# A tiny Exp as ScalarE's first work, with the loads of x and gate_w issued behind it

## Chip, cores and metric

One Trainium2 chip (trn2), one of its cores. The metric is device microseconds of one execution, lower is better. Each kernel is executed several times; of most kernels here some runs are 1.1 to 1.6 us longer than the rest (state "slow"). A profile is one further execution, with its own span; the time of an execution is about 1.7 us longer than the span of its profile.

## The reference, cut to what matters

One decode step mixes two branches with a scalar gate: attention of 32 heads over the last 4096 positions of a K and V cache with 8 heads, and a gated MLP.

```python
x = A_x                                              # (1, 1, 512)
g = _sigmoid((x * gate_w).sum(-1, keepdims=True))
a = attention(x @ wq, k_cache[:, :, -4096:], v_cache[:, :, -4096:]) @ wo
b = (_sigmoid(x @ w_gate) * (x @ w_up)) @ w_down
return g * a + (1 - g) * b
```

Everything is bf16 and read once: wq 4 MB, K and V 8 MB each, wo 4 MB, the three MLP matrices 1.8 MB each. x and gate_w have 1 KB each.

## The kernel before

SyncE issues all big loads in one fixed order, ScalarE the two small ones. A tile pool takes room in SBUF in the order in which its tiles are named, and the pools stand one behind the other, `const` first.

```python
const = ctx.enter_context(tc.tile_pool(name="const", bufs=1))
big = ctx.enter_context(tc.tile_pool(name="big", bufs=1))     # wq, later wo
blk = ctx.enter_context(tc.tile_pool(name="blk", bufs=4))     # four K tiles, later four V tiles
w14 = ctx.enter_context(tc.tile_pool(name="w14", bufs=3))     # w_gate, w_up, w_down
# ... ktp, work and the PSUM pools
xr = const.tile([1, 2, D], BF16, name="xr")
nc.scalar.dma_start(xr[:, 0, :], A_x[0, :, :])
nc.scalar.dma_start(xr[:, 1, :], gate_w.rearrange("(o n) -> o n", o=1))
dq = nc.sync
wq_sb = big.tile([P, DC, HQ * DH], BF16, name="wq_sb", tag="big")
dq.dma_start(wq_sb[:], wq_v)
# ... K, w_gate, w_up, V, wo, w_down, all on dq in this order
spare = const.tile([1, 1], F32, name="spare")
for _ in range(4):
    nc.vector.memset(spare[:], 0.0)
# ... x transposed on TensorE, then the gate:
nc.vector.tensor_tensor(gpr[:], xr[:, 0, :], xr[:, 1, :], op=ALU.mult)
nc.vector.tensor_reduce(gsum[:], gpr[:], axis=AX.X, op=ALU.add)
nc.tensor.matmul(z_ps[:], lhsT=ones_f[0:1, :], rhs=gsum[:], start=True, stop=True)
nc.scalar.activation(gex[:], z_ps[:], AF.Exp, scale=-1.0)     # the first Exp
# ... q = x @ wq on TensorE, K transposed on VectorE, scores, softmax, P V, output projections
```

## Time and profile before

| | before |
|---|---|
| median of 6 runs | 80.65 us (80.44 to 81.89) |
| span of the profile | 78.7 us |
| DMA engines, queue of SyncE | 92.9% of the span, 30.67 MB |
| TensorE, VectorE, ScalarE busy | 67%, 49%, 14% |
| table load for Exp | 1.53 to 2.81 us |
| first Exp | 10.54 us |

To read it: the DMA stream is the bound, and compute follows it at a distance of about a microsecond at the end. The prediction shows the lines.

### The profile page before, as it was taken

What the parts mean: (1) busy time and instruction counts of PE and PEld (TensorE: products, weight loads), DVE (VectorE), ACT (ScalarE), POOL (GpSimd) and SP (SyncE); (2) the same over time, 40 slices, a digit from 0 to 9 for tenths busy, and PEclk for the clock granted to TensorE, in tenths of its full rate; (3) what the DMA queues carried; (4) which work ended last, traced back from release to release, by engine and by line L of the source; (5) the groups of instructions that cost most, each with busy time, mean ns of one, the idle gap of its engine ahead of it and who ended that gap; (6) DMA issues with size and microseconds to landing.
All of it is one profiled execution on the core that took longest, in us unless ns stands there. A gap on an engine that the chain in (4) does not pass through costs nothing.

```text
span 78.7 us, 798 instructions
## 1 busy us (share of the span) xinstructions
PE 52.5 (67%) x314; PEld 23.6 (30%) x314; DVE 38.8 (49%) x52; ACT 10.9 (14%) x20; POOL 3.3 (4%) x10
## 2 busy tenths in 40 slices
PE   0200094999905788898887307999996799567650
PEld 0200041344302333333332202344341345345420
DVE  1600920029869999999986349962000000690020
ACT  2400000247651000000002191000000002000010
POOL 7900000000000000000000000000000000000000
PEclk9999999999999999999999995699999999999997
DMA  7779799999999999999999999999999999999710
GB/s 184 300 316 533 316 483 391 408 425 458 441 408 416 425 474 416 386 437 417 438 410 426 441 416 441 408 433 441 416 433 433 424 425 433 416 391 409 290 42 1
DMA packets 2616, 30.71 MB, mean 390 GB/s; under 512 B 307, under 2 KB 438, under 8 KB 822
## 3 DMA queue, kind: packets, MB, share of 16 engines
q1 hardware_dynamic: 2608, 30.67, 92.9%
q8 instruction: 2, 0.03, 0.2%
q10 hardware_dynamic: 6, 0.00, 0.0%
HBM read 30.67 MB, written 0.00 MB: 390 GB/s over the span
## 4 chain that ended last, share of the span: by engine, by line
DMA 93%; SPq 2%; PE 1%; DVE 1%; issue 0%
DMA wd_sb<-in_B_w_down_dram 36%; DMA kn<-in_A_k_cache_dram 32%; DMA vv<-in_A_v_cache_dram 24%; SPq L84 2%; PE a_ps L290 1%; DVE res L341 1%; SPq L80 0%
## 5 line engine op out<-in xcount | busy, mean ns | idle before, releaser
L299 PE MATMUL pv_ps<-vv,eT 128*32 128x512 bf16 x64 | 15.9, 405 | 4.1 <-DVE eT L271 2.8
L227 PE MATMUL S_ps<-kT,qbig 128*128 128x512 bf16 x64 | 15.2, 378 | 5.0 <-DVE qbig L216 2.8
L188 DVE STREAM_TRANSPOSE kT<-kn 128x2048 f32<-128x2048 f32 x8 | 17.8, 2282 | 0.0
L227 PEld LDWEIGHTS <-qbig 128*128 128x128 bf16 x64 | 6.1, 97 | 14.1 <-issue 4.2
L299 PEld LDWEIGHTS <-eT 128*32 128x32 bf16 x64 | 6.2, 102 | 12.9 <-issue 4.2
L200 PE MATMUL q_ps<-wq_sb,xT 128*128 128x512 bf16 x32 | 8.8, 442 | 1.2 <-DMA wq_sb<-in_A_wq_dram 1.2
L318 DVE TENSOR_TENSOR oT<-o_ps,rb 128x32 bf16<-128x32 f32 x1 | 0.2, 191 | 13.5 <-PE o_ps L316 13.5
L205 DVE STREAM_TRANSPOSE qtT<-q_sb 128x512 f32<-128x512 f32 x4 | 2.7, 700 | 6.9 <-ACT q_sb L202 6.9
L182 PE MATMUL S_ps<-ident,other 2*128 2x512 bf16 x4 | 2.0, 611 | 5.8 <-DVE other L140 5.8
L202 ACT CAST q_sb<-q_ps 128x512 bf16<-128x512 f32 x8 | 4.7, 585 | 7.0 <-PE q_ps L200 7.0
L200 PEld LDWEIGHTS <-xT 128*128 128x128 bf16 x32 | 3.5, 111 | 6.8 <-issue 4.2
L290 PE MATMUL a_ps<-wo_sb,oY 128*1 128x256 bf16 x64 | 3.8, 272 | 1.5 <-DMA wo_sb<-in_A_wo_dram 1.2
L290 PEld LDWEIGHTS <-oY 128*1 128x1 bf16 x64 | 2.7, 83 | 3.1 <-issue 1.4
L271 DVE STREAM_TRANSPOSE eT<-e_sb 128x1024 bf16<-128x1024 bf16 x2 | 2.4, 1224 | 1.9 <-ACT e_sb L269 1.9
L254 ACT ACTIVATE sge<-gu_ps 128x448 f32<-128x448 f32 x1 | 0.5, 543 | 18.9 <-PE gu_ps L243 18.9
L309 ACT COPY pv_sb<-pv_ps 128x512 f32<-128x512 f32 x1 | 0.6, 585 | 17.7 <-PE pv_ps L299 17.7
L341 DVE CAST res<-a_ps 1x256 bf16<-1x256 f32 x1 | 0.4, 412 | 5.2 <-PE a_ps L290 5.2
L281 DVE RECIPROCAL sg<-sge 128x448 f32<-128x448 f32 x1 | 3.0, 2952 | 0.0
L165 DVE TENSOR_TENSOR gpr<-xr 1x512 f32<-1x512 bf16 x1 | 0.7, 679 | 4.6 <-DMA xr<-in_gate_w_dram 4.6
L249 DVE TENSOR_REDUCE pm<-S_ps 128x1 f32<-128x1024 f32 x2 | 2.4, 1208 | 0.9 <-PE S_ps L227 0.9
L290 PE MATMUL a_ps<-wd_sb,hT 128*1 128x256 bf16 x28 | 2.1, 271 | 0.8 <-DMA wd_sb<-in_B_w_down_dram 0.8
L148 PE MATMUL xt_ps<-ident,xr 1*128 1x1 bf16 x4 | 0.3, 165 | 3.5 <-POOL ident L126 3.5
(62 smaller groups left out, 31.0 us busy)
## 6 DMA issues: line engine op xcount, KB each, us to landing
kn<-in_A_k_cache_dram SPq DMA_DIRECT2D x4, 2048.0 KB, 27.2
vv<-in_A_v_cache_dram SPq DMA_DIRECT2D x4, 2048.0 KB, 19.1
wq_sb<-in_A_wq_dram SPq DMA_DIRECT2D x1, 4096.0 KB
wo_sb<-in_A_wo_dram SPq DMA_DIRECT2D x2, 2048.0 KB
wg_sb<-in_B_w_gate_dram SPq DMA_DIRECT2D x1, 1792.0 KB
wu_sb<-in_B_w_up_dram SPq DMA_DIRECT2D x1, 1456.0 KB
wd_sb<-in_B_w_down_dram SPq DMA_DIRECT2D x1, 1024.0 KB
wd_sb<-in_B_w_down_dram SPq DMA_DIRECT2D x1, 384.0 KB
```

What stands on the lines that cost most here:

```text
L84: dq.dma_start(t[:, n0:n1, :].rearrange("p n d -> p (n d)"), cache[0, 2 * a:2 * a + 2, SBASE:SBASE + W, :] .rearrange("y (x n) d -> x y n ...
L182: nc.tensor.matmul(S_ps[u // 2][:, u % 2, :], lhsT=other[:].rearrange("p o y u -> p (o y u)"), rhs=ident[0:2, 0:2].rearrange("p (o y) -> p ...
L188: nc.vector.transpose(t[:].bitcast(F32), kn[a][:, v * KB:(v + 1) * KB, :] .rearrange("p n d -> p (n d)").bitcast(F32))
L200: nc.tensor.matmul(q_ps[:], lhsT=xT[:, c:c + 1].to_broadcast([P, P]), rhs=wq_sb[:, c, ks], start=(c == 0), stop=(c == DC - 1))
L202: nc.scalar.copy(q_sb[:, ks], q_ps[:])
L205: nc.vector.transpose(qtT[:].bitcast(F32)[:, kq], q_sb[:].bitcast(F32)[:, kq])
L227: nc.tensor.matmul(S_ps[v][:, hb, :], lhsT=q_st[:, a, dhi, :, t], rhs=k_v[:, hb * 16:(hb + 1) * 16, dhi, :, t], start=False, stop=(a == HP ...
L249: nc.vector.tensor_reduce(pm2[:, v:v + 1], S_ps[v][:].rearrange("p a b -> p (a b)"), axis=AX.X, op=ALU.max)
L271: nc.vector.transpose(eT[:, :, v * KB:(v + 1) * KB, :].rearrange("p a n r -> p n a r"), e_sb[:, v, :].rearrange("p (n a r) -> p n a r", a= ...
L281: nc.vector.reciprocal(sg[:], sge[:])
L290: nc.tensor.matmul(a_ps[32 * i:32 * i + 1, i, 0:HN], lhsT=lhsT, rhs=rhs[:, i * HN:(i + 1) * HN], start=start, stop=stop)
L299: nc.tensor.matmul(pv_ps[32 * a:32 * a + 32, :, :], lhsT=eT[:, a, 4 * m:4 * m + 4, :].rearrange("p n r -> p (n r)"), rhs=vv[a][:, 4 * m:4 ...
```

## The change

ScalarE is put under the written order from the start, and its first instruction is an Exp on a one-element tile, so that the table of Exp is loaded while nothing else is to be done. The loads of x and gate_w come behind it.

```diff
+    ctx.enter_context(tc.manual_schedule(engines={mybir.EngineType.Activation}))
+    warm = const.tile([1, 1], F32, name="warm")
+    nc.vector.memset(warm[:], 0.0)
+    nc.scalar.activation(warm[:], warm[:], AF.Exp)
     xr = const.tile([1, 2, D], BF16, name="xr")
     nc.scalar.dma_start(xr[:, 0, :], A_x[0, :, :])
     nc.scalar.dma_start(xr[:, 1, :], gate_w.rearrange("(o n) -> o n", o=1))
@@
-    for _ in range(4):
+    for _ in range(3):
         nc.vector.memset(spare[:], 0.0)
```

## The prediction

> **What bounds the kernel now.** I began with the slices of the page and its queue table, to see which resource has no room left.
>
> ```profile
> DMA  7779799999999999999999999999999999999710
> ...
> q1 hardware_dynamic: 2608, 30.67, 92.9%
> ```
>
> The first line gives the busy share of the 16 DMA engines in 40 slices of the 78.7 us span: 7 to 9 tenths up to slice 6, then 9 without a gap until slice 37. In the second line the queue that SyncE fills carries 30.67 MB and takes 92.9% of the engines. No compute engine is near this (PE 67%, DVE 49%). Next came the chain of waits in order of time (start us, duration, what).
>
> ```profile
> 46.84 28.67 DMA wd_sb<-in_B_w_down_dram
> 75.51 0.04 issue
> 75.55 0.66 PE a_ps L290 x6
> 76.20 0.40 DVE res L341
> ```
>
> The last piece of compute, 0.66 us of matmuls and a 0.40 us copy, follows the landing of the last part of w_down at 75.51 us. Before it the chain consists of transfers alone (93% of the span on the page). So the end is set by how long one queue needs for its bytes, plus about 1.1 us of compute and the store. A change at the start matters only if it makes this stream start earlier or later, makes it run dry, or holds compute up for longer than compute now waits for data.
>
> To see which work the change touches, I read the timeline of the first 20 us (start, duration, engine, line, tiles, count, and in brackets the idle time before it with its releaser).
>
> ```profile
> 0.73 0.38 SPq L80 DMA_DIRECT2D wq_sb<-in_A_wq_dram  x1
> 0.74 0.51 ACTq L74 DMA_DIRECT2D xr<-in_A_x_dram  x1
> ...
> 1.28 0.21 ACTq L75 DMA_DIRECT2D xr<-in_gate_w_dram  x1
> ...
> 1.53 1.28 ACT L170 ACT_TABLE_LOAD   x1 [1.53 <-PEq L358]
> 2.03 1.25 DVE L153 COPY xp<-xr 1x64 bf16<-1x64 bf16 x2 [0.83 <-DMA xr<-in_A_x_dram]
> ...
> 7.83 0.68 DVE L165 TENSOR_TENSOR gpr<-xr 1x512 f32<-1x512 bf16 x1 [4.56 <-DMA xr<-in_gate_w_dram]
> ...
> 9.55 0.14 DVE L158 CAST xT<-xt_ps 128x4 bf16<-128x4 f32 x1
> ...
> 9.68 0.60 PE L182 MATMUL S_ps<-ident,other 2*128 2x512 bf16 x1 [5.75 <-DVE other L140]
> ...
> 10.37 1.44 PE L182 MATMUL S_ps<-ident,other 2*128 2x512 bf16 x3
> 10.54 0.17 ACT L170 ACTIVATE gex<-z_ps 128x1 f32<-128x1 f32 x1 [7.73 <-PE z_ps L168]
> ...
> 12.98 7.25 PE L200 MATMUL q_ps<-wq_sb,xT 128*128 128x512 bf16 x25 [1.17 <-DMA wq_sb<-in_A_wq_dram]
> ```
>
> Three things are to be seen. First, the table load for Exp already stands at 1.53 us, right behind the two small loads, and ends at 2.81; the first Exp starts at 10.54 and the page of waits puts its 7.7 us of idle time on z_ps, a matmul. The load has 7.7 us to spare. Second, the x load, issued at 0.74, lets VectorE start at 2.03, while gate_w, issued half a microsecond later, releases gpr only at 7.83. Third, everything between gate_w and the first q matmul runs in VectorE's and TensorE's order: gpr, its sum, two small setup instructions and xT, then four matmuls that end at 11.81 (10.37 + 1.44). The q matmuls then wait 1.17 us for wq, until 12.98.
>
> Why gate_w takes 6.3 us (1.49 to 7.83) is told by the trace's packet records. Both loads are one packet of 1024 bytes and one of 4 bytes, on one DMA engine. The data packet of x went at 1.64, before that engine began on wq at 1.76. The data packet of gate_w went at 6.21, behind three wq packets of 32 KB (2.0, 1.23 and 1.22 us), and its 4-byte packet at 7.47, exactly one wq packet later.
>
> For the slack further on I read the later timeline.
>
> ```profile
> 27.70 14.67 SPq L84 DMA_DIRECT2D vv<-in_A_v_cache_dram  x4
> ...
> 61.58 2.97 PE L299 MATMUL pv_ps<-vv,eT 128*32 128x512 bf16 x13 [1.28 <-DMA vv<-in_A_v_cache_dram]
> ...
> 71.38 1.91 PE L290 MATMUL a_ps<-wo_sb,oY 128*1 128x256 bf16 x32 [1.22 <-DMA wo_sb<-in_A_wo_dram]
> ...
> 73.90 1.46 PE L290 MATMUL a_ps<-wd_sb,hT 128*1 128x256 bf16 x22 [0.61 <-DMA wd_sb<-in_B_w_down_dram]
> ...
> 75.55 0.61 PE L290 MATMUL a_ps<-wd_sb,hT 128*1 128x256 bf16 x6 [0.19 <-DMA wd_sb<-in_B_w_down_dram]
> ```
>
> Here PE waits for data at vv (1.28 us), at the second half of wo (1.22), and at two parts of w_down (0.61 and 0.19).
>
> **What the Trainium skill says.** "ScalarE: Activation LUTs", section "What ACT_TABLE_LOAD costs", gives about 1283 ns for the load and about 1380 ns of drain; the trace has 1283 ns for the load and cannot show the drain, as ScalarE has nothing to do behind it. "DMA: Bandwidth & Descriptors", section "Queues, rings and completion order", says that each DMA engine takes turns between queues at packet granularity; the one wq packet between gate_w's two packets agrees, the three before the first one are more than a single turn, and I take the measured three. "Perfetto Trace Analysis", section "DVE / Act Engine Instruction (TENSOR_ADD, Activation, etc)", says that the sequencer pushes an instruction into a wait queue and is then ready for the next; whether the loads therefore pass the running table load is shown nowhere in this trace. "TensorE: Matmul & The Clock Gate", Part 1, puts the slow phase of a cold TensorE at about 3.4 us of activity; here q matmuls are 0.43 us apart from 12.98 to 16.35, 3.37 us, and about 0.22 apart afterwards.
>
> **The change, part by part.** The diff looks like a gain of one table load. I compared the instruction orders of the two builds as well.
>
> Removed: one of four VectorE memsets (four take 0.40 us at 0.79) in place of which the memset of the warm tile comes. Net zero, and VectorE has 0.83 us of idle time there. The table load of gex moves to the front; as the Exp at 10.54 waited for a matmul, nothing is gained on that side.
>
> Added: one 1x1 Exp, estimated at 0.17 us after the 128x1 Exp of gex (171 ns).
>
> Moved: the loads of x and gate_w. If the sequencer goes on while the table loads, x is issued just after the memset, at about 1.0 us. If it waits for the Exp, at 0.74 + 1.28 + 0.17, about 2.2. If a drain of 1.38 us is paid as well, at about 3.6. Issue takes 0.51 us and the packet went 0.39 us behind it (1.25 to 1.64). So x reaches its DMA engine at about 1.9, 3.1 or 4.5. In none of these is it ahead of wq, whose first packet there started at 1.76. With the running packet and two more ahead, as for gate_w, the first two cases put the data of x at 6.2 and the third at 7.45. From there one wq packet (1.22) lies between each two of the four small packets: the last, of gate_w, comes 3.7 us after the first, at 9.9 or 11.1, and lands 0.36 us later (7.47 to 7.83): 10.3 or 11.5. That is 2.5 to 3.7 us later than now.
>
> From gate_w's landing to the end of the setup matmuls is 11.81 - 7.83 = 3.98 us, so q can start at 14.3 or 15.5, against 12.98: 1.3 or 2.5 us late, since 1.17 us are swallowed by the wait for wq. Part of this returns. The setup matmuls now join the q matmuls without the 1.17 us gap, so I estimate that the 3.37 us of slow pace begin with them: in the first case from 12.15, until 15.5, when some 3 q matmuls are done, and the other 29 at 0.216 need 6.3 us, to about 21.8. Now the last q matmul ends at about 21.7. So compute behind q is late by 0.1 us, in the other case by about 1.3, and if the warm-up doesn't help, by the full 1.3 or 2.5.
>
> What lies behind q has room for this: 1.28 + 1.22 + 0.61 + 0.19 = 3.3 us of waits for data on PE. So the end of compute doesn't move.
>
> Does the stream move? The order of SyncE's queue is unchanged. In the build, the semaphores that DMAs share in turn rotate by one: wq now comes before x, so the load of w_up, which waited for x, now waits for wq. Its issue goes from 4.47 to about 12.95. At that moment four K loads of 2 MB and 1.8 MB of w_gate are still queued, about 24 us at the measured 0.41 to 0.43 MB per us. The V loads, issued at 27.70 and later, also wait for VectorE to free the K buffers. The first such transpose ends 24.52 + 2.27 = 26.8, so 0.9 us of lateness is free; beyond this a V load would be issued up to 1.6 us late, with some 5.6 MB (13 us) queued before it. The queue never runs dry. Without the x issue beside it, the wq issue may be a little shorter; at most 0.1 us, an estimate.
>
> Sum: 0 on the end, perhaps -0.1.
>
> **The rivals.** (1) The load hides nothing now and the early Exp makes the kernel faster. For it: 2.66 us by the skill. Against it: 7.7 us of ScalarE waiting for z_ps, and a stream-bound end. It would give 78 us only if ScalarE were in the chain, which it isn't. (2) Late x and gate_w delay q beyond the slack. It needs gate_w to land after 7.83 + 1.17 + 3.3 = 12.3 us, without any help from the warm-up; my worst case is 11.5, and the wq packets in front end at 12.1. One or two more packets ahead would give 12.7 or 13.9, so 81 to 82.3 us. For it: the depth of three packets rests on one observation. Against: even then most of it is absorbed. (3) The K buffers are freed late and the stream runs dry. That would need V issues over 13 us late; it would cost the lateness beyond this. I rule it out.
>
> **Range and chances.** The three runs before are 80.44, 80.73 and 81.89; the third is over 1.5% above the fastest, so I take the mean of the other two, 80.6, as its fast time, and nothing added: 80.6 us. The low end is 0.5 us below, for spread and a quicker first issue. The high end is 0.9 above, for a gate_w that lands a packet or so later than my worst case. Faster by over 2% (below 79.0) would need fewer bytes or a quicker stream: 0.02. Slower by over 2% (above 82.2) needs gate_w past 13.9 us: 0.04. Within: 0.94.
>
> **What would show it.** In the changed profile: the table load at about 0.75 us; VectorE's xp copies moved from 2.03 to about 7.8 to 9; gpr at 10.3 to 11.5; the idle time of the first q matmul put on the setup instructions in place of wq, its start at 14.3 to 15.5; w_up issued near 12.95; the waits for vv and wo on PE shorter; the DMA slices still 9 up to the end and the last landing of w_down at 75.4 to 75.6. I am wrong if the last landing moves by over 0.5 us, if the last waits of PE for w_down are gone and the chain of the end runs through VectorE or PE, or if x still lands near 2 us.

## The result, and the profile after

The changed kernel takes 79.81 us in the median of six runs (79.54 to 80.04), the kernel before 80.65. The ratio is 0.9906, with a 95% interval of 0.9879 to 0.9934. A ratio here is the mean time of one kernel's fast runs over that of the other's from the same rounds (79.80 over 80.56), so not quite the ratio of the medians. The change is under 2%, as said, but the time lies below my range: 0.76 us (80.56 less 79.80) have gone that I did not foresee.

The slices and the queue of SyncE on the page of the kernel after look the same:

```profile
DMA  6789798999999999999999999999999999999810
...
q1 hardware_dynamic: 2608, 30.67, 92.9%
```

The chain of waits (start us, duration, what) has the same pieces, and its end comes earlier. The transfer at its end is the third of the four parts of w_down, not the last, as the prediction has it; it landed at 75.51 us and lands now at 74.93:

```profile
46.60 28.32 DMA wd_sb<-in_B_w_down_dram
74.93 0.04 issue
74.97 0.63 PE a_ps L294 x6
75.60 0.40 DVE res L345
```

The six matmuls behind it include two that wait for the fourth part. By the semaphore records of the trace that part landed at 75.84 us before and lands at 75.24 now. So 0.60 us of the 0.64 us between the two spans (78.74 and 78.10) had been gained when the last load landed. The compute pieces are as long as before to a few hundredths (0.63 and 0.40 us; 0.66 and 0.40 before). The start of the timeline (start, duration, engine, line, tiles, count, idle time before):

```profile
0.73 1.28 ACT L76 ACT_TABLE_LOAD   x1 [0.73 <-PEq L362]
...
0.89 0.50 ACTq L78 DMA_DIRECT2D xr<-in_A_x_dram  x1
...
2.02 0.20 ACT L76 ACTIVATE warm<-warm 1x1 f32<-1x1 f32 x1
...
5.56 0.33 DVE L157 COPY xp<-xr 1x64 bf16<-1x64 bf16 x2 [4.45 <-DMA xr<-in_A_x_dram]
...
8.04 0.68 DVE L169 TENSOR_TENSOR gpr<-xr 1x512 f32<-1x512 bf16 x1 [2.15 <-DMA xr<-in_gate_w_dram]
...
10.75 0.17 ACT L174 ACTIVATE gex<-z_ps 128x1 f32<-128x1 f32 x1 [8.53 <-PE z_ps L172]
...
13.23 0.33 SPq L103 DMA_DIRECT2D wu_sb<-in_B_w_up_dram  x1
13.25 9.46 PE L204 MATMUL q_ps<-wq_sb,xT 128*128 128x512 bf16 x32 [1.24 <-DMA wq_sb<-in_A_wq_dram]
```

The table load runs from 0.73 to 2.01 us, and ScalarE issues x at 0.89, in the middle of it: its queue doesn't wait for the load or for the Exp at 2.02. x lands 3.5 us later than before (VectorE starts at 5.56 in place of 2.03). gate_w lands at almost the same time (gpr at 8.04 in place of 7.83), and the first q matmul still waits for wq, 1.24 us. Nothing that q waits for has become earlier. The later timeline answers to the last lines of the prediction:

```profile
61.21 2.97 PE L303 MATMUL pv_ps<-vv,eT 128*32 128x512 bf16 x13 [0.69 <-DMA vv<-in_A_v_cache_dram]
...
70.92 1.91 PE L294 MATMUL a_ps<-wo_sb,oY 128*1 128x256 bf16 x32 [1.13 <-DMA wo_sb<-in_A_wo_dram]
...
73.36 2.20 PE L294 MATMUL a_ps<-wd_sb,hT 128*1 128x256 bf16 x28 [0.53 <-DMA wd_sb<-in_B_w_down_dram]
```

V, wo and w_down each arrive some 0.4 to 0.6 us earlier, and PE still waits for each of them. The gain lies in the stream itself, somewhere between 13 us, when wq lands in both kernels, and the end.

**Where in the stream.** The profile's GB/s come out at 430 in both kernels from 45 to 60 us, which is too coarse. The packet records of the trace are finer. A packet here is one record of the trace: one row of a load. Every big load has 128 of them and 16 small ones for the semaphore that tells of its landing, so 8 rows for each of the 16 engines. Apart from those of wq and a few single ones of some 0.5 us more, packets of one size in one stretch take the same time to within a few ns:

```
mean ns of a packet                     before   after
K, 13 to 24 us       (16384 bytes)       611.0   611.0
K, 27 to 31 us       (16384 bytes)       615.5   611.0
w_gate               (14336 bytes)       540.9   535.0
w_up                 (11648 bytes)       444.2   436.0
V, 45 to 64 us       (16384 bytes)       615.6   611.0
first packets above 611 ns, sustained     25.5   none
```

Up to 25 us the two kernels are alike. Then the packets of the kernel before take 0.7% longer to the end. Summed per engine over all loads, the excess over the changed kernel's packets is 0.26 us in K, V and wo, 0.05 in w_gate, 0.07 in w_up and 0.09 in w_down, 0.47 us together. That is most of the 0.60 us. What could make all packets slower was not in my prediction at all, so the experiments start from the parts of the change.

### The profile page after: what moved, and what is told of

It is laid out like the page before. It is cut to its first block, busy times and chain, and to the rows that moved or that the text cites. A ratio compares the mean times of both kernels' runs of the same rounds, so it can differ in the third digit from the quotient of the medians.

```text
span 78.1 us, 799 instructions
## 1 busy us (share of the span) xinstructions
PE 53.6 (69%) x314; PEld 23.9 (31%) x314; DVE 37.9 (48%) x52; ACT 11.1 (14%) x21; POOL 3.3 (4%) x10
## 4 chain that ended last, share of the span: by engine, by line
DMA 93%; SPq 2%; PE 1%; DVE 1%; issue 0%
DMA wd_sb<-in_B_w_down_dram 36%; DMA kn<-in_A_k_cache_dram 32%; DMA vv<-in_A_v_cache_dram 24%; SPq L88 2%; PE a_ps L294 1%; DVE res L345 1%; SPq L84 0%
## 5 line engine op out<-in xcount | busy, mean ns | idle before, releaser
L231 PE MATMUL S_ps<-kT,qbig 128*128 128x512 bf16 x64 | 16.3, 404 | 3.9 <-DVE qbig L220 2.8
L303 PE MATMUL pv_ps<-vv,eT 128*32 128x512 bf16 x64 | 15.2, 411 | 3.5 <-DVE eT L275 2.8
L204 PE MATMUL q_ps<-wq_sb,xT 128*128 128x512 bf16 x32 | 9.5, 468 | 1.2 <-DMA wq_sb<-in_A_wq_dram 1.2
```

The lines of the kernel that those rows point to most:

```text
L204: nc.tensor.matmul(q_ps[:], lhsT=xT[:, c:c + 1].to_broadcast([P, P]), rhs=wq_sb[:, c, ks], start=(c == 0), stop=(c == DC - 1))
L231: nc.tensor.matmul(S_ps[v][:, hb, :], lhsT=q_st[:, a, dhi, :, t], rhs=k_v[:, hb * 16:(hb + 1) * 16, dhi, :, t], start=False, stop=(a == HP ...
L303: nc.tensor.matmul(pv_ps[32 * a:32 * a + 32, :, :], lhsT=eT[:, a, 4 * m:4 * m + 4, :].rearrange("p n r -> p (n r)"), rhs=vv[a][:, 4 * m:4 ...
```

## The experiments

All ratios are to the kernel before, run in the same rounds, with five rounds each.

**The two kernels again.** No edit; is the packet rate a property of the kernels or of the two executions that were profiled?

> The kernel before, against itself. Its only profile has K and V packets of 16 KB that take 611 ns up to 25 us and 612 to 621 ns from there to the end. Theory A (the lower packet rate belongs to this kernel): ratio 1.00, and packets from 26 us on again at about 614 ns. Theory B (the rate is a matter of the single profile, not of the kernel): ratio 1.00 too, but packets at 611 ns throughout, with a span of some 78.3 us.

> The changed kernel once more. Theory A: ratio 0.99 and 16 KB packets at 611 ns throughout. Theory B: ratio still 0.99 if the gain has another cause than the packet rate; packets may be at 614 ns in this profile. If the gain was chance of the chip that was drawn: ratio 1.00.

The kernel before against itself gave 1.0007 (0.9993 to 1.0021), with packets at 615.5 ns from 25.4 us on, and the changed kernel 0.9936 (0.9918 to 0.9953), with 611.0 ns to the end. The rate belongs to the kernel.

**The Exp behind the loads.**

```diff
     warm = const.tile([1, 1], F32, name="warm")
     nc.vector.memset(warm[:], 0.0)
-    nc.scalar.activation(warm[:], warm[:], AF.Exp)
     xr = const.tile([1, 2, D], BF16, name="xr")
     nc.scalar.dma_start(xr[:, 0, :], A_x[0, :, :])
     nc.scalar.dma_start(xr[:, 1, :], gate_w.rearrange("(o n) -> o n", o=1))
+    nc.scalar.activation(warm[:], warm[:], AF.Exp)
```

> The changed kernel with the Exp behind the two loads: same tiles, same addresses, same early table load for ScalarE in all but order, x again ahead of wq. If the gain comes from the loads being late or from the DMA semaphores being rotated: ratio 1.00. If it comes from the shifted addresses of all tiles behind the new one, or from the Exp itself: ratio 0.99.

0.9938 (0.9921 to 0.9955): the whole gain without the order that the change is about. Its profile fell in a slow run, so I take from it only that its K packets stay at 611 ns between 27 and 31 us.

**A late x without Exp.**

```diff
     xr = const.tile([1, 2, D], BF16, name="xr")
+    nc.vector.memset(xr[:], 0.0)
     nc.scalar.dma_start(xr[:, 0, :], A_x[0, :, :])
@@
-    for _ in range(4):
+    for _ in range(3):
```

> The kernel before with a VectorE memset of the x tile ahead of the loads, so that x is issued some tenths of a microsecond later and lands behind wq packets, with the semaphores rotated as in the changed kernel, but with no early Exp and no new tile. If the gain comes from the loads being late or from the rotation: ratio 0.99 and x landing near 5.5 us. If from the Exp or the addresses: ratio 1.00.

1.0012 (1.0000 to 1.0025), packets at 615.4 ns from 25 us on. The moved loads and the rotated semaphores make no gain. This kernel, by the way, is the one that my prediction described; x came later than I expected of this run, behind three wq packets. From its timeline:

```profile
10.41 0.68 DVE L166 TENSOR_TENSOR gpr<-xr 1x512 f32<-1x512 bf16 x1 [2.15 <-DMA xr<-in_gate_w_dram]
...
14.32 9.14 PE L201 MATMUL q_ps<-wq_sb,xT 128*128 128x512 bf16 x32
...
28.59 0.58 SPq L85 DMA_DIRECT2D vv<-in_A_v_cache_dram  x1
```

gpr starts at 10.41 and q at 14.32, where I had 10.3 and 14.3 for the changed kernel. V is first issued 0.9 us later than before (27.70). And the chain of waits shows that none of it reaches the end (the same part of w_down landed at 75.51 before, and at 75.45 when that kernel was run again):

```profile
75.54 0.04 issue
75.58 0.65 PE a_ps L291 x6
76.23 0.40 DVE res L342
```

**Addresses alone.** What is left of the change is the new tile. It takes 32 bytes of every partition ahead of all others. In the builds, the first K buffer moves from byte 63200 to 63232 of a partition, and all big tiles move with it: from 32 bytes past a multiple of 64 (224 past a multiple of 256) to a multiple of 256. The next two kernels take the two halves of the change apart.

```diff
+    pad = const.tile([1, 8], F32, name="pad")          # pad32: 32 bytes
+    nc.vector.memset(pad[:, 0:1], 0.0)
     xr = const.tile([1, 2, D], BF16, name="xr")
@@
-    for _ in range(4):
+    for _ in range(3):
```

> The kernel before, with a 32-byte tile allocated ahead of xr and one of the four spare memsets writing it; no early Exp, x issued as before. All big tiles then start at the addresses of the changed kernel (the first K buffer at byte 63232 of a partition, a multiple of 64 and of 256, in place of 63200). If the addresses make the gain: ratio 0.993, 16 KB packets at 611 ns to the end. If the Exp makes it: ratio 1.00 and packets at 614 ns from 25 us on.

```diff
+    wlast = ctx.enter_context(tc.tile_pool(name="wlast", bufs=1))   # warm_last, on the changed kernel: a pool behind all others
-    warm = const.tile([1, 1], F32, name="warm")
+    warm = wlast.tile([1, 1], F32, name="warm")
```

> The changed kernel with its warm tile in a pool of its own behind all others, so that every other tile lies at the address of the kernel before. Exp first, loads behind it, semaphores rotated as in the changed kernel. If the addresses make the gain: ratio 1.00 and packets at 614 ns from 25 us on. If the Exp makes it: ratio 0.993 and packets at 611 ns.

The padding alone gives 0.9915 (0.9898 to 0.9933) and packets at 611.0 ns. The early Exp with late loads and the old addresses gives 1.0003 (0.9986 to 1.0019) and packets at 615.5 ns. The ends of the two chains of waits, pad32 first and warm_last second, show the same half microsecond as the two kernels of the change (the last part of w_down landed at 75.37 and 75.89 us):

```profile
75.04 0.04 issue
75.08 0.65 PE a_ps L292 x6
```

```profile
75.56 0.04 issue
75.60 0.66 PE a_ps L295 x6
```

**How much alignment.** Three kernels differ from pad32 in the size of the tile only.

```diff
-    pad = const.tile([1, 8], F32, name="pad")           # pad32
+    pad = const.tile([1, 16], F32, name="pad")          # pad64; [1, 24] in pad96, [1, 40] in pad160
```

> As pad32 with a 64-byte tile: the addresses move by 64, so the first K buffer is at 63264, again 32 bytes off a multiple of 64. If alignment to 64 bytes or more decides: ratio 1.00, packets at 614 ns. If any move of the addresses does (a clash of one buffer with something): ratio other than 1.00, 0.993 for instance.

> As pad32 with a 96-byte tile: the first K buffer is at 63296, a multiple of 64 but of neither 128 nor 256. If 64 bytes decide: ratio 0.993, packets at 611 ns. If 128 or 256 bytes decide: ratio 1.00, packets at 614 ns.

> As pad32 with a 160-byte tile: the big tiles start at multiples of 128 that are not multiples of 256 (the first K buffer at 63360). So far: 32 bytes off a multiple of 64 gave packets of 615.5 ns on average from 25 us on, a multiple of 64 alone 614.8 ns from 28.7 us on, a multiple of 256 gave 611 ns. If 128 bytes are enough: ratio 0.992, 611 ns throughout. If 256 are needed: ratio 0.998 to 1.00 and an average between 612 and 615 ns, from later than 28.7 us on.

```
start of the big tiles             ratio (95% interval)      K, 27-31   V, 45-64   sustained from
32 past a multiple of 64 (before)  1.0007 (0.9993-1.0021)     615.5      615.6     25.4 us
32 past a multiple of 64 (pad64)   0.9994 (0.9980-1.0009)     615.5      615.6     25.6 us
multiple of 64 only (pad96)        0.9982 (0.9961-1.0002)     612.1      614.8     28.7 us
multiple of 128 only (pad160)      0.9968 (0.9943-0.9993)     611.2      614.6     29.8 us
multiple of 256 (pad32)            0.9915 (0.9898-0.9933)     611.0      611.0     none
```

Of the starts tried, only multiples of 256 give the full pace. In the packets, multiples of 64 and 128 alone help a little, and the loss begins later; in time this is small (0.9968 for 128) or not clear of noise (the interval for 64 reaches 1.0002). (pad96's profile fell in a slow run; its packets can be read, its span can't.) The move alone does nothing: pad64 moves everything by 64 bytes and leaves the time as it was. align_all, below, has the full gain at a second address that is a multiple of 256.

The Trainium skill has a page that bears on this, and I had not connected it with a tile of one element. "DMA: Bandwidth & Descriptors", section "How a descriptor splits into AXI transactions", says that a transfer is cut into transactions of 256 B which must start at 256 B boundaries; by that rule 16384 bytes that start elsewhere need 65 in place of 64 (an estimate from the page). The measured boundary of 256 agrees. The page's count of extra beats (units of 32 B) doesn't set the size: by its rule a start 32 bytes past a boundary (pad64) costs 1 extra beat and one 224 bytes past (before) costs 7 (estimates too), and both have 615.6 ns. The packets of w_up speak for the number of transactions: 11648 bytes from 224 past a boundary touch 47 stretches of 256 B and take 444.2 ns (before); from 32 past they touch 46, as from a multiple of 256, and take 437.3 (pad64, without one packet of 900 ns; 436.0 in the changed kernel). No run was made to test this. And the page speaks of reads, while here the source addresses are the same in all kernels and only the SBUF side moved.

**Which tiles, and why only from 25 us.** The last question is why the packets of badly aligned K loads (starts that are no multiple of 256) run at full pace for 13 us. Two kernels split the tiles, with padding in pools of their own between `big`, `blk` and `w14`; each padding tile is written in place of one of the four spare memsets.

```diff
     big = ctx.enter_context(tc.tile_pool(name="big", bufs=1))
+    pad_bp = ctx.enter_context(tc.tile_pool(name="pad_b", bufs=1))   # 32 bytes in both
     blk = ctx.enter_context(tc.tile_pool(name="blk", bufs=4))
+    pad_cp = ctx.enter_context(tc.tile_pool(name="pad_c", bufs=1))   # 224 bytes in kv_off, 32 in rest_off
     w14 = ctx.enter_context(tc.tile_pool(name="w14", bufs=3))
# kv_off also has the 32-byte pad of pad32 ahead of xr
```

> Only the K and V buffers lie 32 bytes off a multiple of 64; wq, w_gate, w_up, wo and w_down lie at multiples of 256. Theory T (each packet to a badly aligned buffer is slow from some moment near 25 us on): the last K load and all V loads at 615.5 ns, w_gate at 535 and wo at 611 ns, ratio about 0.996. Theory F (the writing side falls behind by 4.5 ns per 16 KB packet from the start, and the packets show it once a store of about 170 ns, that is some 38 packets, is full; an estimate from the onset in the two slow alignments): K packets at 611 ns to their end, as 32 packets make 146 ns, w_gate at 535 ns, V at 611 ns if the store empties meanwhile; ratio 0.993.

> The reverse: K and V buffers at multiples of 256, all the weights 32 bytes off a multiple of 64. Theory T: w_gate at 539 to 540 ns and w_up at 444, wo at 615.5, V at 611 ns; ratio about 0.997. Theory F: wq fills the store by 73 ns and the K loads may empty it, w_gate and w_up add some 60 ns, the V loads empty it again, wo and w_down add some 130 ns: no packet slower than in the changed kernel; ratio 0.992.

kv_off gave 0.9935 (0.9902 to 0.9968), rest_off 0.9940 (0.9910 to 0.9970). Packet times, and the lag, which is the time from a load's last semaphore packet to its landing on the semaphore:

```
mean ns                  before   after   kv_off   rest_off
K, 27 to 31 us            615.5   611.0    613.2    611.0
w_gate                    540.9   535.0    536.0    535.0
V, 45 to 64 us            615.6   611.0    614.8    611.0
us, last packet to landing
wq                         0.33    0.32     0.32     0.31
first K load               0.36    0.29     0.33     0.29
second K load              0.39    0.28     0.37     0.33
third K load               0.42    0.33     0.41     0.31
fourth K load              0.42    0.33     0.43     0.28
w_gate                     0.43    0.28     0.40     0.32
third V load               0.46    0.32     0.49     0.35
```

Theory T, that each badly aligned packet is slow from some moment on, falls with rest_off: its w_gate lies badly and has 535 ns where T wants 539, and wo has 611 where T wants 615.5. Theory F fits in its idea and is wrong in two of its figures (K at 613.2 and V at 614.8 ns in kv_off, where it has 611). The landing falls behind the packets by 0.03 to 0.04 us with each badly aligned K load, which is 8 packets times the 4.5 ns by which they are slow later (36 ns). When it is some 0.1 us behind, it stays there, and from that moment the packets themselves are slow: after 2.7 K loads in the kernel before, after 3.2 in kv_off. The reading that fits is that the writing side is slow from the first badly aligned K packet, and that the packet records show the reading side and hide it until something between the two, a store, is full. It is inferred from the lags; no record here shows the two sides apart. I had estimated a store of 170 ns filled from wq on; by the loads counted it is nearer 100 ns (2.7 and 3.2 times 36 are 97 and 115), and wq adds next to nothing (its lag is 0.33 us badly aligned and 0.32 well aligned). A third case agrees: in rest_off wo's 16 packets per engine (16 times 4.5 ns, 72 ns) run at 611 ns, and only the last parts of w_down behind them are slow (85.1 ns in place of 84.0 for those of 2048 bytes). Well aligned loads empty the store, but slowly: in kv_off V still starts slow after w_gate and w_up, which ran at full pace (w_gate from its fourth packet on), and the lag is back at 0.33 us only at the last part of w_down (0.30 in the changed kernel, 0.48 in the one before). Why wq with its packets of 32 KB adds so little, and what the store is, stays open.

**All tiles aligned.**

```diff
+    pad = const.tile([1, 32], F32, name="pad")          # align_all: xr and the small w_up tile at multiples of 256 too
+    nc.vector.memset(pad[:, 0:1], 0.0)
     xr = const.tile([1, 2, D], BF16, name="xr")
@@
+    pad_w = const.tile([1, 40], F32, name="pad_w")      # and the big tiles again
+    nc.vector.memset(pad_w[:, 0:1], 0.0)
     spare = const.tile([1, 1], F32, name="spare")
-    for _ in range(4):
+    for _ in range(2):
```

> The kernel before with xr, the small w_up tile and all big tiles at multiples of 256, no early Exp, x issued as before. If the alignment of the big tiles is all there is to gain: ratio 0.992, as pad32 and the changed kernel. If the small transfers gain as well: a little lower, 0.990 at best.

0.9914 (0.9886 to 0.9941), with a mean of the fast runs of 79.79 us: as pad32 (79.80) and the changed kernel (79.80). The small transfers add nothing that these rounds resolve, and no kernel here beats the changed one; pad32 equals it without any Exp.

## Why the prediction was wrong, step by step

**The bound** held: the stream ends the kernel before and after (chain of waits), and PE waits for V, wo and w_down in both. One reading was wrong: 75.51 us is the landing of the third part of w_down, and the last landed at 75.84, within the 0.66 us of matmuls that the prediction took for compute alone.

**"Does the stream move? ... nothing added: 80.6 us"** is the step that failed. I asked of the stream only whether its order, its issue times and its queue change, and took its pace for given. I compared instructions of the two builds, not the addresses. The runs show in its place: a tile of 4 bytes, which takes 32, moves every big DMA destination from 32 bytes past a multiple of 64 to a multiple of 256; 16 KB packets go from 615.6 to 611.0 ns from 25 us on (0.47 us in sum over all loads), and the landing loses the extra lag behind the packets (0.43 to 0.28 us for w_gate, 0.46 to 0.32 for the third V load). At the end the last semaphore packet starts 0.43 us earlier (75.37 to 74.94) and its lag shrinks from 0.48 to 0.30: together the 0.60 us by which the last load lands earlier. So the prediction's first sign of being wrong, a last landing that moves by over 0.5 us, is what came. pad32 shows the move of the addresses alone, warm_last shows the rest of the change to be worth nothing. The step "perhaps -0.1" for a quicker wq issue was empty: the wq issue takes 0.38 us in both kernels.

**The table load**: right. It was hidden and is hidden; gex starts at 10.75 in place of 10.54 and waits for z_ps as before. "Perfetto Trace Analysis" is borne out on the point that I left open: the sequencer went on, and x was issued at 0.89 while the load ran.

**How late x and gate_w are**: right in the spacing, wrong in the start. The four small packets went at 3.93, 5.21, 6.42 and 7.67 us, one wq packet apart as read from gate_w before. But the first had one wq packet ahead of it, not three, so xp came at 5.56 and not after 7.8, gpr at 8.04 and not at 10.3, and q at 13.25, still waiting for wq and not for the setup. In late_x, issued half a microsecond later, it was three again (6.32). How many packets lie ahead depends on more than I read from one case.

**The slack**: right. late_x uses it, and has the predicted 14.3 for q, V issued late, and the same end; so rivals (2) and (3) did not come about. The changed kernel uses some of it too: its q matmuls took 9.46 us, against 8.76 before, the first S matmul starts at 25.47 in place of 24.50, and PE's wait for V shrinks from 1.28 to 0.69 us. My estimate that the setup matmuls would shorten the slow pace of q was not borne out: the q matmuls of late_x took 9.14 us. Nor is the 3.37 us of slow pace fixed: it lasted 5.0 us in the changed kernel, 5.9 in pad32 and 3.3 when the kernel before was run again.

**w_up's issue**: right, 13.23 us against "near 12.95", without effect.

**The range**: its low end allowed for scatter and a quicker first issue only. A mechanism that speeds the stream was in none of the rivals, so 79.81 fell below 80.1. That the time would stay within 2% was right by luck: the argument for it was that nothing moves the stream, and what did move it happened to be worth 0.9%.

## What to carry to other kernels

When a change names a new tile, compare the addresses of the two builds before giving its effect to the instructions, and try the change once with the new tile behind all others. In a kernel bound by its loads, try to start the big destination tiles at multiples of 256 bytes of the partition; a few bytes of padding are enough to do it, and here they were the whole gain (0.9915 in pad32). Packet records can keep a steady rate while the landings fall behind, here for 13 us, so look at landings as well.

## What the Trainium skill lacked or had wrong

- "SBUF — State Buffer", section "Operand start alignment", treats alignment as a question of legality and says that its runs timed nothing. Here the start of a DMA destination within its partition is worth 0.7% of the pace of a 16 KB packet (615.6 against 611.0 ns), and of the starts tried only multiples of 256 give the full pace.
- "DMA: Bandwidth & Descriptors", section "How a descriptor splits into AXI transactions", gives the boundary of 256 B for what a transfer reads. It lacks the SBUF side of a load, and its beats don't scale the cost of a 16 KB packet there (32 and 224 bytes past a boundary: 615.6 ns both; 64 and 128 bytes past: 614.8 and 614.6).
- No page says how far the packets of a load into SBUF can run ahead of its landing: here the lag grew from 0.33 us at wq to 0.39 to 0.42 over the first two to three K loads, before the packets became slower.
- The same DMA page, section "Queues, rings and completion order", says that a DMA engine takes turns between queues packet by packet, and gives a packet several descriptors. Here, in records of one row each, a small load on another queue found one row of the big load ahead of it in the changed kernel and three in two other cases; only the spacing between the small packets was one row. Whether such a record is a packet in the page's sense is not shown, so this may be a gap of the page and no error.
